# The opening of a fused attention and expert kernel: one-bank products, finer weight transfers, early first products

## Chip, cores, metric

One core of a Trainium2 chip. The metric is device time of one execution in microseconds (us). Ratios are the mean time of one kernel's fast runs over that of the kernel before in the same rounds, so they are not quite the ratios of the medians that stand beside them.

## The reference

```
q_s = softmax(q, over head dim);  k_s = softmax(k, over sequence)
x   = q_s @ (k_s^T @ v)              # batch 8, heads 8, sequence 576, head dim 64
h   = x @ w_in                       # 4608 tokens, 512 model dims, 2048 hidden columns
g   = h + sin(alpha * h)^2 / alpha
out = g @ w_out                      # (4608, 512), f32
```

Inputs are f32; the kernel multiplies in bf16.

## The kernel before

PE (TensorE) makes everything from tiles of 512 tokens: attention for a batch gives x^T; then 16 groups of 128 hidden columns ("hidden column 0 to 15" below), each four products of w_in with x^T, one per 128 model dims; then the output products from g and w_out. ACT (ScalarE) makes sines and some squares, POOL (GpSimd) and DVE (VectorE) the other squares, DVE the sums g. q, k, v of batch 0 come by SyncE's queue; the weights by POOL's queue, which casts them f32 to bf16, and behind them q, k, v of batch 1.

```python
def load_win(c0, c1):
    n = slice(c0 * 512, c1 * 512)
    for x in range(2):
        nc.gpsimd.dma_start(out=win[64 * x:64 * x + 64, :, n], in_=win_v[x][:, :, n])
...
    warm_up(14)                       # identity products, to bring the clock up
    norm_q(0, [GP, V])
    for c0, c1 in ((0, 1), (1, 2), (2, 4)):
        load_win(c0, c1)
    for c in range(3):
        load_wout(c)
    ...                               # casts of v, transposes of q
    for ii in range(2):
        kv_mm(0, ii, ps_s, split=True)
        kv_norm(0, ii, ii + 1)
    for ii in range(2):
        attn_out(0, ii, 0, ps_s, (ACT_CP, DVE_CP)[ii])
        attn_out(0, ii, 1, ps_s, (ACT_CP, DVE_CP)[ii])
        warm_up((1, 4)[ii])
...
    late = {3: ("q", q, 1, True), 6: ("k", k, 1, False), 8: ("v", v, 1, True)}
    for ni in range(nN):
        h_slot(0, ni, "PAPDPAPADPAPPDAP"[ni], lag, lent)   # A, P, D: who squares
        flush(lag, 1)                                      # DVE's sum, one behind
        if ni in late: ...            # load of batch 1, by POOL's queue
        if ni == 11:
            load_wout(3)
```

The softmax here doesn't subtract the row's maximum and nothing guards it: scores larger than these inputs give would overflow.

## Time and profile before

| | before |
|---|---|
| time, median of three runs | 293.79 us (293.63 to 294.30) |
| PE busy, share of the span | 278.9 us, 96% |
| first product of tile 0 | 17.38 us |
| last part of w_in landed | 24.20 us |
| first product of tile 1 | 49.58 us |

With a fourth run the median is 293.94, which the tables below use. PE has almost no idle time after the opening, so a change of the opening shows at the end as the shift of tile 1's first product: in all fourteen profiles of this case the span less that moment is 241.8 to 242.2 us.

### The profile page before, as it was taken

The page shows a single profiled execution, that of the slowest core. Times are in us where ns is not written, and L with a number is a line of the kernel's source. Part 1 is how long each engine was busy: PE and PEld are TensorE (multiplying, and loading weights), DVE is VectorE, ACT ScalarE, POOL GpSimd, SP SyncE. Part 2 cuts the span into 40 slices and gives each one's busy share as a digit, 9 for nine tenths or more (in the row PEclk, how much of TensorE's full clock was granted, in tenths as well). Part 3 has the DMA queues.
Part 4 walks back from the last instruction along what each step waited for, and adds up shares of the span by engine and source line. Part 5 has one row for each costly group of instructions (what it writes and reads, how often), then busy time and mean ns, then how long its engine had stood idle before and what let it go on. Part 6 is the DMA issues. An engine that isn't in the chain of part 4 may idle for free.

```text
span 291.4 us, 4261 instructions
## 1 busy us (share of the span) xinstructions
PE 278.9 (96%) x1576; PEld 132.4 (45%) x1576; DVE 188.0 (65%) x275; ACT 226.7 (78%) x320; POOL 84.9 (29%) x78
## 2 busy tenths in 40 slices
PE   2999999999999999999999999999999999999994
PEld 1444445444454445444444444445444444444444
DVE  3748955798958667855786568756774555555412
ACT  4679956999579899789987998799977777777500
POOL 0939571576684744002600070005000000000000
PEclk9999999999999999999999999999999999999999
DMA  7999999964899975109920894113411111111143
GB/s 260 294 181 207 357 254 339 395 226 130 208 139 374 393 239 117 37 23 334 290 55 14 290 292 97 36 39 70 83 38 36 36 36 38 36 36 37 38 108 73
DMA packets 35253, 45.77 MB, mean 157 GB/s; under 512 B 15888, under 2 KB 19744, under 8 KB 35232
## 3 DMA queue, kind: packets, MB, share of 16 engines
q1 hardware_dynamic: 29632, 34.09, 41.3%
q0 software_dynamic: 5408, 11.27, 15.4%
q8 instruction: 12, 0.20, 0.3%
q10 hardware_dynamic: 192, 0.14, 0.2%
q14 instruction: 9, 0.07, 0.1%
HBM read 36.71 MB, written 9.44 MB: 158 GB/s over the span
## 4 chain that ended last, share of the span: by engine, by line
PE 80%; DVE 8%; ACT 5%; POOL 3%; issue 2%; DMA 1%; ACTq 0%
PE op L255 35%; PE hp L235 31%; PE hp L255 4%; DVE g L251 3%; PE warm L299 2%; PE kvp L154 2%; POOL s L245 2%; DVE xT L215 2%; ACT s L241 2%; PE xp L212 2%; DMA st_q<-in_q_dram 1%; PE op L498 1%; PE hh L235 1%; ACT s L243 1%; DVE o L261 1%
## 5 line engine op out<-in xcount | busy, mean ns | idle before, releaser
L251 DVE SCALAR_TENSOR_TENSOR g<-s,inva_sb,hp 128x512 bf16<-128x512 f32 x130 | 95.3, 746 | 64.6 <-ACT s L243 52.1
L235 PE MATMUL hp<-xT,win 128*128 128x512 bf16 x520 | 129.5, 379 | 0.2
L255 PE MATMUL op<-wout,g 128*128 128x512 bf16 x496 | 124.0, 379 | 0.0
L241 ACT ACTIVATE s<-hp,alpha_sb 128x512 f32<-128x512 f32 x130 | 87.8, 682 | 29.4 <-PE hp L235 25.4
L235 PEld LDWEIGHTS <-win 128*128 128x128 bf16 x576 | 56.1, 98 | 68.1 <-issue 1.9
L255 PEld LDWEIGHTS <-g 128*128 128x128 bf16 x560 | 54.1, 98 | 62.6 <-issue 1.5
L243 ACT ACTIVATE s<-s 128x512 f32<-128x512 f32 x112 | 70.5, 629 | 3.6
L143 POOL TENSOR_TENSOR qn<-qe,qs 128x1152 bf16<-128x1152 bf16 x13 | 27.4, 2127 | 83.7 <-DVE qs L137 67.6
L245 POOL TENSOR_TENSOR s<-s 128x512 f32<-128x512 f32 x27 | 28.4, 1058 | 23.6 <-ACT s L241 23.4
L261 DVE COPY o<-op 128x512 f32<-128x512 f32 (+1 forms) x33 | 21.9, 664 | 10.1 <-PE op L255 7.6
L114 ACT ACTIVATE ke<-st_k 128x1152 bf16<-128x1152 f32 x16 | 17.7, 1149 | 3.2 <-DMA st_k<-in_k_dram 3.2
L114 ACT ACTIVATE qe<-st_q 128x1152 bf16<-128x1152 f32 x16 | 17.9, 1156 | 2.9 <-DMA st_q<-in_q_dram 2.9
L136 DVE TENSOR_REDUCE qs<-qe 128x36 f32<-128x2304 bf16 x5 | 12.8, 2553 | 10.8 <-ACT qe L114 10.7
L128 POOL CAST vb<-st_v 128x1152 bf16<-128x1152 f32 x14 | 16.1, 1175 | 8.7 <-DMA st_v<-in_v_dram 8.6
L215 DVE CAST xT<-xp 128x512 bf16<-128x512 f32 (+1 forms) x22 | 16.5, 752 | 2.8 <-PE xp L212 2.7
L255 PE MATMUL hp<-wout,g 128*128 128x512 bf16 x64 | 15.1, 379 | 0.4 <-DVE g L251 0.3
L212 PE MATMUL xp<-qT,kbd 128*128 128x256 bf16 (+1 forms) x56 | 10.8, 285 | 2.1 <-DVE xT L215 1.0
L154 PE MATMUL kvp<-vb,ke 64*128 64x130 bf16 x288 | 9.8, 216 | 0.5 <-ACT qT L187 0.4
L114 ACT ACT_TABLE_LOAD x7 | 9.0, 1283 | 1.3 <-PEq L514 1.2
L154 PEld LDWEIGHTS <-ke 64*128 64x128 bf16 x288 | 8.2, 93 | 3.8 <-issue 2.1
L299 PE MATMUL warm<-qe,identb 128*128 128x512 bf16 x19 | 7.4, 554 | 2.7 <-ACT qe L114 2.7
L212 PEld LDWEIGHTS <-kbd 128*128 128x128 bf16 x56 | 5.3, 97 | 9.2 <-issue 3.8
(59 smaller groups left out, 121.3 us busy)
## 6 DMA issues: line engine op xcount, KB each, us to landing
out_dram<-o SPq DMA_DIRECT2D x70, 128.0 KB, 2.4
st_q<-in_q_dram SPq DMA_DIRECT2D x5, 1152.0 KB, 6.1
st_k<-in_k_dram SPq DMA_DIRECT2D x5, 1152.0 KB, 8.7
st_v<-in_v_dram SPq DMA_DIRECT2D x5, 1152.0 KB, 10.9
st_k<-in_k_dram POOLq DMA_DIRECT2D x2, 1152.0 KB, 11.1
wout<-in_moe_w_out_dram POOLq DMA_DIRECT2D x4, 512.0 KB, 14.6
st_q<-in_q_dram SPq DMA_DIRECT2D x2, 576.0 KB, 4.4
st_k<-in_k_dram SPq DMA_DIRECT2D x2, 576.0 KB, 7.1
```

Source lines behind the costliest of these rows:

```text
L114: nc.scalar.activation(dst[:, :, ii * 128:(ii + 1) * 128].rearrange("p j (x d) -> p x j d", x=2), src[:, ii::2], AX.Exp)
L143: engs[ii % len(engs)].tensor_tensor(qn[:, ii].rearrange("p j (x d) -> p j x d", x=2), qe[:, ii], part.unsqueeze(3).to_broadcast([128, J, ...
L154: nc.tensor.matmul(kvp[:, e, ii * 130:(ii + 1) * 130], ke[r, j, ii * 128:(ii + 1) * 128], vt[r, j, ii * 130:(ii + 1) * 130], start=(j == 0 ...
L212: nc.tensor.matmul(xp[:, e, 0:n], kt[:, e, ii], qT[:, ii, j0:j1, e * 64:(e + 1) * 64], start=True, stop=True)
L215: eng(xT[:, 2 * ii:2 * ii + 2, c0:c0 + n], xp[:, :, 0:n])
L235: nc.tensor.matmul(hp, win[:, ki, ni * 128:(ni + 1) * 128], xT[:, ki, t * MF:(t + 1) * MF], start=(ki == 0), stop=(ki == 3))
L241: nc.scalar.activation(s, hp, AX.Sin, scale=alpha_sb[:, ni:ni + 1])
L243: nc.scalar.activation(s, s, AX.Square)
L245: nc.gpsimd.tensor_tensor(s, s, s, op=ALU.mult)
L251: nc.vector.scalar_tensor_tensor(G[t][:, ni], in0=s, scalar=inva_sb[:, ni:ni + 1], in1=hp, op0=ALU.mult, op1=ALU.add)
L255: nc.tensor.matmul(acc, G[t][:, ni, j * 128:(j + 1) * 128], wout[:, ni, :], start=(ni == 0), stop=(ni == nN - 1))
L261: eng(o[:, cols], acc)
```

## The change

Intent: begin the tile-0 products sooner. Batch 0's attention is made for the first 512 tokens alone, in four one-bank products (each into a PSUM tile of 128x512 f32 instead of 128x2x512), one for each quarter of the model dims; the first two hidden columns start on the first quarters while the others are still copied; w_in comes in finer column parts so that the first columns are there (`load_win` now counts columns, not blocks of 512); the squares of tile 0 are dealt out anew; and in batch 1 the last w_out chunk goes between the halves of v, whose casts move from POOL to ACT and DVE. The diff, cut to its core:

```diff
-        warm_up(14)
+    warm_up(9)
...
-        for c0, c1 in ((0, 1), (1, 2), (2, 4)):
+    for c0, c1 in ((0, 256), (256, 512), (512, 1024), (1024, 2048)):
         load_win(c0, c1)
-        for c in range(3):
+    for c in range(2):
         load_wout(c)
...
-        for ii in range(2):
-            attn_out(0, ii, 0, ps_s, (ACT_CP, DVE_CP)[ii])
-            attn_out(0, ii, 1, ps_s, (ACT_CP, DVE_CP)[ii])
-            warm_up((1, 4)[ii])
+    for c in range(4):
+        xp = ps_h.tile([128, MF], F32, name="hp", tag="h")
+        attn_chunk(0, c, 0, 8, xp)
+        (ACT_CP, ACT_CP, DVE_CP, ACT_CP)[c](xT[:, c, 0:MF], xp)
...
-        late = {3: ("q", q, 1, True), 6: ("k", k, 1, False), 8: ("v", v, 1, True)}
+        late = {3: lambda: load("q", q, 1, halves=True, eng=GP), 5: lambda: load_wout(2),
+                7: lambda: load("k", k, 1, eng=GP), 9: lambda: load_half("v", v, 1, 0, GP),
+                11: lambda: load_wout(3), 12: lambda: load_half("v", v, 1, 1, GP)}
+        for ki in range(2):
+            for ni in range(2):
+                mm_h(0, ni, lent, ki, ki + 1)
         for ni in range(nN):
-            h_slot(0, ni, "PAPDPAPADPAPPDAP"[ni], lag, lent)
+            h_slot(0, ni, "DAPPAPPDAPPDAPAP"[ni], lag, lent)
...
+        take(os, 10)
+        for c in range(4):
+            attn_chunk(0, c, 8, 9, xp[:, c])      # the last 64 tokens of batch 0
+        ACT_CP(xT[:, :, 8 * P:9 * P], xp)
+        take(os, 36)
         exp_q(1); norm_q(1, [GP, V]); exp_k(1)
-        cast_v(1, [GP_CP, GP_CP])
+        cast_v(1, [ACT_CP, DVE_CP])
```

More of the change, by code (lines that the diff above doesn't have):

```diff
@@ L94, in load, with load_half @@
         staged[name, b] = st
+    def load_half(name, t, b, ii, eng):
+        if ii == 0:
+            staged[name, b] = stage.tile([128, 4, J, D], F32, name=f"st_{name}", tag="st")
+        eng.dma_start(out=staged[name, b].rearrange("p i j d -> p i (j d)")[:, ii::2], in_=src_view(t, b)[:, ii::2])
     def load_batch(b):
@@ L101, in load_win @@
     def load_win(c0, c1):
-        n = slice(c0 * 512, c1 * 512)
+        n = slice(c0, c1)
         for x in range(2):
@@ L168, in kv_norm @@
                                     kvr[r, :, :, x].unsqueeze(3).to_broadcast([64, 2, m, D]), op=ALU.mult)
-    TP = ((0, 6), (6, 9))
     def q_tile(b):
@@ L175, in q_tile, with q_transpose @@
         return A["qT", b]
-    def q_transpose(b, g, pool, eng):
-        qn, qT = A["qn", b], q_tile(b)
-        j0, j1 = TP[g]
-        m = (j1 - j0) // 3
-        tp = pool.tile([128, 2, 2, 4, 128], BF16, name="tp", tag="a")
-        for j in range(j0, j1):
-            h, jj = divmod(j - j0, 3)
-            for ii in range(2):
-                nc.tensor.transpose(tp[:, h, ii, jj], qn[:, ii, j], identb)
-        for ii in range(2):
-            eng(qT[:, ii, j0:j1].rearrange("p (h jj) c -> p h jj c", h=m), tp[:, 0:m, ii, 0:3])
+    def q_transpose(b, ii, pool, eng):
+        tp = pool.tile([128, 16, 128], BF16, name="tp", tag="a")
+        q_transpose_ii(b, ii, 0, J, tp)
+        eng(q_tile(b)[:, ii], tp[:, 0:J])
     def q_transpose_ii(b, ii, j0, j1, tp):
@@ L224, with mm_h @@
     G = {}
-    def mm_h(t, ni, wide=None):
-        if ni == 0:
+    HP = {}
+    def mm_h(t, ni, wide=None, k0=0, k1=4):
+        if ni == 0 and k0 == 0:
             G[t] = gpool.tile([128, nN, MF], BF16, name="g")
-        if wide and ni % 6 in ((2, 3) if t == 0 else (4, 5)):
+        if k0:
+            hp = HP[t, ni]
+        elif wide and ni % 6 in ((2, 3) if t == 0 else (4, 5)):
             hp = wide()
@@ L233, in mm_h @@
             hp = ps_h.tile([128, MF], F32, name="hp", tag="h")
-        for ki in range(4):
+        HP[t, ni] = hp
+        for ki in range(k0, k1):
             nc.tensor.matmul(hp, win[:, ki, ni * 128:(ni + 1) * 128],
@@ L284 @@
         nc.vector.memset(vb[n].rearrange("p j (i c) -> p j i c", i=4)[:, :, :, D:D + 1], 1.0)
-    with tc.tile_pool(name="ps_w", bufs=1, space=PSUM) as ps_w, tc.tile_pool(name="ps_s", bufs=3, space=PSUM) as ps_s:
-        warm = ps_w.tile([128, 4, 128], F32, name="warm")
-        tpa = warm[:, 0, 0:nN]
-        nc.tensor.transpose(tpa, alpha_rows, ident[0:nN, 0:nN])
-        DVE_CP(alpha_sb, tpa)
-        nc.vector.reciprocal(inva_sb, alpha_sb)
-        exp_q(0)
-        exp_k(0)
-        def warm_up(n):
-            for _ in range(n):
-                nc.tensor.matmul(warm, identb, A["qe", 0][:, 0:4, 0:128], start=True, stop=True)
-        def cast_v0(n, eng):
-            ii, j0, j1 = VJ[n]
-            vv = vb[0].rearrange("p j (i c) -> p i j c", i=4)
-            eng(vv[:, 2 * ii:2 * ii + 2, j0:j1, 0:D], staged["v", 0][:, ii::2, j0:j1])
-        warm_up(14)
-        norm_q(0, [GP, V])
-        for c0, c1 in ((0, 1), (1, 2), (2, 4)):
-            load_win(c0, c1)
-        for c in range(3):
-            load_wout(c)
-        cast_v0(0, ACT_CP)
-        cast_v0(1, DVE_CP)
-        q_transpose(0, 0, ps_s, ACT_CP)
-        q_transpose(0, 1, ps_s, DVE_CP)
-        cast_v0(2, DVE_CP)
-        for ii in range(2):
-            kv_mm(0, ii, ps_s, split=True)
-            kv_norm(0, ii, ii + 1)
-        for ii in range(2):
-            attn_out(0, ii, 0, ps_s, (ACT_CP, DVE_CP)[ii])
-            attn_out(0, ii, 1, ps_s, (ACT_CP, DVE_CP)[ii])
-            warm_up((1, 4)[ii])
-        nc.scalar.activation(zero, zero, AX.Sin)
@@ L326 @@
-    ps_h = ctx.enter_context(tc.tile_pool(name="ps_h", bufs=4, space=PSUM, reuse_waits="tile"))
+    ps_h = ctx.enter_context(tc.tile_pool(name="ps_h", bufs=4, space=PSUM, reuse_waits="tile"))
+    ES = ExitStack()
+    ps_e = ES.enter_context(tc.tile_pool(name="ps_e", bufs=2, space=PSUM, reuse_waits="tile"))
+    tps = [ps_h.tile([128, 8, 128], BF16, name="tp", tag="h") for _ in range(3)]
+    warm = ps_h.tile([128, 4, 128], F32, name="warm", tag="h")
+    tpa = warm[:, 0, 0:nN]
+    nc.tensor.transpose(tpa, alpha_rows, ident[0:nN, 0:nN])
@@ new lines, with warm_up, cast_v0 @@
+    DVE_CP(alpha_sb, tpa)
+    nc.vector.reciprocal(inva_sb, alpha_sb)
+    exp_q(0)
+    exp_k(0)
+    def warm_up(n):
+        for _ in range(n):
+            nc.tensor.matmul(warm, identb, A["qe", 0][:, 0:4, 0:128], start=True, stop=True)
+    def cast_v0(ii, j0, j1, eng):
+        vv = vb[0].rearrange("p j (i c) -> p i j c", i=4)
+        eng(vv[:, 2 * ii:2 * ii + 2, j0:j1, 0:D], staged["v", 0][:, ii::2, j0:j1])
+    warm_up(9)
+    norm_q(0, [GP, V])
+    q_tile(0)
+    for c0, c1 in ((0, 256), (256, 512), (512, 1024), (1024, 2048)):
+        load_win(c0, c1)
@@ new lines @@
+    for c in range(2):
+        load_wout(c)
+    q_transpose_ii(0, 0, 0, 8, tps[0])
+    DVE_CP(A["qT", 0][:, 0, 0:8], tps[0])
+    cast_v0(0, 0, 5, ACT_CP)
+    cast_v0(0, 5, 9, DVE_CP)
+    warm_up(1)
+    q_transpose_ii(0, 1, 0, 8, tps[1])
+    for ii in range(2):
+        q_transpose_ii(0, ii, 8, 9, tps[2][:, ii:ii + 1])
+    ACT_CP(A["qT", 0][:, :, 8], tps[2][:, 0:2])
+    cast_v0(1, 0, 5, DVE_CP)
+    ACT_CP(A["qT", 0][:, 1, 0:8], tps[1])
+    cast_v0(1, 5, 9, ACT_CP)
+    for ii in range(2):
+        kv_mm(0, ii, ps_e, split=True)
+        kv_norm(0, ii, ii + 1)
@@ L328, in h_slot @@
+    for c in range(4):
+        xp = ps_h.tile([128, MF], F32, name="hp", tag="h")
+        attn_chunk(0, c, 0, 8, xp)
+        (ACT_CP, ACT_CP, DVE_CP, ACT_CP)[c](xT[:, c, 0:MF], xp)
+    nc.scalar.activation(zero, zero, AX.Sin)
     def h_slot(t, ni, sq, lag, wide=None):
-        hp = mm_h(t, ni, wide)
+        hp = mm_h(t, ni, wide, 2 if t == 0 and ni < 2 else 0)
         lag.append((t, ni, hp, sine(t, ni, hp, sq)))
@@ L356 @@
     SQ = "PAPDPAPAPPDPAPAP"
-    with tc.tile_pool(name="ps_e", bufs=2, space=PSUM, reuse_waits="tile") as ps_e:
+    with ES:
         def lent():
             return ps_e.tile([128, 2, MF], F32, name="hh", tag="a")[:, 0]
-        late = {3: ("q", q, 1, True), 6: ("k", k, 1, False), 8: ("v", v, 1, True)}
+        late = {3: lambda: load("q", q, 1, halves=True, eng=GP), 5: lambda: load_wout(2),
[4 more added lines that the diff above has]
+                mm_h(0, ni, lent, ki, ki + 1)
         for ni in range(nN):
-            h_slot(0, ni, "PAPDPAPADPAPPDAP"[ni], lag, lent)
+            h_slot(0, ni, "DAPPAPPDAPPDAPAP"[ni], lag, lent)
             flush(lag, 1)
             if ni in late:
-                name, x, b, hv = late[ni]
-                load(name, x, b, halves=hv, eng=GP)
-            if ni == 11:
-                load_wout(3)
+                late[ni]()
         flush(lag, 0)
+        accs = [ps_h.tile([128, dm], F32, name="hp", tag="h") for _ in range(4)]
+        os = o_quad(0, accs, [DVE_CP, ACT_CP, DVE_CP, ACT_CP])
+        take(os, 10)
+        xp = ps_e.tile([128, 4, P], F32, name="xp", tag="a")
+        for c in range(4):
+            attn_chunk(0, c, 8, 9, xp[:, c])
+        ACT_CP(xT[:, :, 8 * P:9 * P], xp)
+        take(os, 36)
         exp_q(1)
@@ L374 @@
         exp_k(1)
-        cast_v(1, [GP_CP, GP_CP])
+        cast_v(1, [ACT_CP, DVE_CP])
         for name, x in (("q", q), ("k", k), ("v", v)):
             load(name, x, 2, eng=GP)
-        accs = [ps_h.tile([128, dm], F32, name="hp", tag="h") for _ in range(4)]
-        os = o_quad(0, accs, [DVE_CP, ACT_CP, DVE_CP, ACT_CP])
-        take(os, 44)
         q_transpose(1, 0, ps_e, ACT_CP)
         nc.scalar.activation(zero, zero, AX.Sin)
-        take(os, 2)
         q_transpose(1, 1, ps_e, DVE_CP)
```

## The prediction

> **What bounds the kernel now.** I read the page first: TensorE (PE) is busy in 96% of the span, in every slice of forty but the first and the last, and the chain that ended last lies 80% on PE. So a gain in the opening is kept to the end only if PE's stream from there on starts earlier. Tile 1 and everything after it has the same instructions in both kernels; the quantity to predict is therefore the moment at which the first product of tile 1 starts, 49.58 us in the profile. Next I read PE's timeline of the opening (start, length, engine, line, what, count, idle before it):
>
> ```profile
> 5.89 5.97 PE L299 MATMUL warm<-qe,identb 128*128 128x512 bf16 x14 [2.66 <-ACT qe L114]
> 11.70 1.17 PE L185 MATMUL tp<-identb,qn 128*128 128x128 bf16 x18
> 12.80 1.54 PE L154 MATMUL kvp<-vb,ke 64*128 64x130 bf16 x36
> ...
> 17.38 1.89 PE L235 MATMUL hp<-xT,win 128*128 128x512 bf16 x8
> 19.10 1.89 PE L235 MATMUL hh<-xT,win 128*128 128x512 bf16 x8
> 20.83 3.62 PE L235 MATMUL hp<-xT,win 128*128 128x512 bf16 x16
> 24.34 1.89 PE L235 MATMUL hh<-xT,win 128*128 128x512 bf16 x8
> ...
> 33.90 7.71 PE L255 MATMUL hp<-wout,g 128*128 128x512 bf16 x35 [0.28 <-DVE g L251]
> ```
>
> The tile-0 products run from 17.38 to 31.24 with no gap of note (64 matmuls at 0.216 us are 13.8 us). It looks as if an earlier start at 17.38 would pay. But the weight loads of the same line, asked for around 24 us, and the view of the w_in tile tell another story:
>
> ```profile
> 23.85 0.10 PEld L235 LDWEIGHTS <-win 128*128 128x128 bf16 x1
> 24.31 0.34 PEld L235 LDWEIGHTS <-win 128*128 128x128 bf16 x3 [0.36 <-issue]
> ```
>
> ```profile
> L104 POOL DMA_DIRECT2D win<-in_moe_w_in_dram x6: 640/661/787, 9.8 to 13.0; - x6
> ...
> DMA to landing us min/median/max: 4.5/7.2/11.2
> ```
>
> The last of six w_in transfers is issued at 13.0 and takes 11.2 us: it lands at 24.2. Hidden column 8 x 128 is the first that needs it, and its weights load at 24.31, 0.1 us after the landing, where the load had the weight path idle for 0.36 us. PE lost only about 0.06 us there, so products and w_in arrive together: PE has no slack against the transfer. The slices of 2 us (length, busy time and count of PE, PEld, DVE, ACT, POOL, then clock, DMA share, GB/s) say why w_in comes so late:
>
> ```profile
> 8.00:10.00 2.00, 2.00 (x6) 0.72 (x5) 1.93 (x3) 1.26 (x2) 2.00 (x2) 1.00 1.05 388
> ...
> 14.00:16.00 2.00, 1.50 (x18) 0.92 (x16) 1.34 (x5) 0.99 (x3) 1.87 (x3) 1.00 1.16 141
> 16.00:18.00 2.00, 1.85 (x10) 0.74 (x9) 1.42 (x2) 1.74 (x3) 0.00 (x0) 1.00 1.09 168
> 18.00:20.00 2.00, 2.00 (x11) 0.91 (x10) 0.00 (x0) 1.37 (x2) 0.79 (x1) 1.00 1.17 215
> ```
>
> The DMA share is about 1 or over in all of them. The weights are counted as bf16 written; their f32 source is twice that, so 205 GB/s written is some 410 read, the same rate as q, k and v before them. By the landings in the trace the queue stays full from w_in through two w_out chunks, the third, batch 1's q, k, v (41.3) and the last w_out chunk (43.67). Batch 1's kv products start at 43.88 and end at 45.07; attn_out follows at 46.31, tile 1 at 49.58. The opening is as much a DMA queue of 41 us as a PE stream.
>
> **What the Trainium skill says.** "DMA: Bandwidth & Descriptors", section "Issuing engines are not separate DMA queues": all transfers share 16 engines whoever issues them. The trace agrees: no rate over about 410 GB/s read, from either queue. Same page, "Why small descriptors are slow (HBM only)": a fixed cost per packet. The packet records agree: 2048 B written took 173 ns, 1024 B took 98, so the fixed part is about 23 ns. "TensorE: Matmul & The Clock Gate", Part 1: half clock until a window of about 3.4 us was busy. In the trace the warm-up products are 426 ns apart until the clock goes to full at 11.57, 5.7 us after the first. "ScalarE: Activation LUTs", "What ACT_TABLE_LOAD costs": 1283 ns; the trace has 1283 too, before the first sine.
>
> **The change part by part.**
>
> *Start of the products.* Five fewer warm-ups take 5 x 0.426 = 2.1 us from PE's queue (9.73 instead of 11.86), so transposes start when qn's halves are there (9.82 and 11.03). v's first half lands at 11.40, its second at 12.27 and 13.01. With casts of 0.44 to 0.7 us split over ACT and DVE, and the long qT copy on ACT ahead of its last cast (13.4 to 13.9), kv of the second half ends near 14.3, kv_norm 0.75 later at 15.05. Four one-bank attention products and four copies of 0.6 to 0.7 us give x^T's quarters at 15.2, 15.8, 16.2 and 16.4. Products of the first model dims start near 15.5, and by 17.1 the first two hidden columns are done, which is 2.0 us ahead of before (17.38 + 1.73 = 19.11). ACT gains only 0.5: its copy still ends at 16.4, the table load takes 1.28, so the first sine comes at 17.9 rather than 18.44.
>
> *w_in parts.* The bytes are the same and the first issue is where it was, behind POOL's normalisation (9.76). The first quarter of the columns now goes in packets of 512 B, about 60 ns each by the two measured sizes: with the overlap seen at 1024 B that is 168 instead of 205 GB/s, so 0.5 MB takes 3.1 us instead of 2.6. The first two hidden columns can be had near 14.3 (w_in's first pair was 15.79), which suits the early start. But columns 1024 to 2048 remain the last pair: 24.2 plus up to 0.5. PE, 2 us early, waits for the second group about 0.9 us near 19 and for the third to 24.3-24.8. The last eight hidden columns are 8 x 0.863 = 6.9 us, so tile 0 ends at 31.2 to 31.8 instead of 31.24. The 2 us do not survive.
>
> *Tile 0's tail.* ACT and DVE catch up during those waits, and the last squares are no longer DVE's (one took 1.48 us beside POOL): the 0.28 us wait at 33.9 goes. Four 64-column products for the last 64 tokens cost 0.2. Before, 44 output products were done at 41.6; now 46 at 41.4 to 42.0: +0.1 to -0.5 in all.
>
> *Batch 1.* The third w_out chunk moves behind q, so q lands 2.5 us earlier, but its exp waits for the extra copy and table load, about 35.5, later than the 33.84 of before; qn is still there (near 41.8) when its transposes come. v's second half is now last in the queue, behind the last w_out chunk. The queue's end was 43.67; call the new landing L. Its cast moves from POOL (1.2 us) to DVE (0.75 by 0.44 for 512 and 0.50 for 640 columns), then in DVE's order the 1152-column qT copy (0.9) and kv_norm (1.1): attention products can start at L + 2.85 and tile 1 3.27 after that (46.31 to 49.58 before), so at L + 6.1. That equals 49.58 at L = 43.5. With L = 43.67 plus 0 to 0.5 the change loses 0.2 to 0.7; PE's own stream, if L were not the limit, would gain about 0.5 at most at the same w_in landing.
>
> Sum: +0.2 to +0.7 us, of 293.8. Against it I set one thing the trace does not explain: from 14.5 to 16.7 the same 1024 B packets took up to 172 ns, while POOL issued the w_out chunks. One chunk fewer is issued there now. If that stretch of low rate shrinks, the whole queue comes up to 1.2 us earlier, and everything with it. I take half a microsecond for it, and a little more for the reordering having been tuned: -0.2 in all, 293.6.
>
> **The rivals.**
> *The opening gain goes through.* If the tile-0 products' 2 us were kept, 291.8. For it: PE's gapless stream and the chain, which names the warm-ups. Against: the landing at 24.2 beside the load at 24.31.
> *The finer parts cost more.* Packets of 512 B at 98 ns would halve the rate of the first quarter: +2.6 us on the queue, so 296. Against it: the source f32 rows are 1 KB, and packets of q and v of that size on the other queue took 50 ns.
> *The clock stays at half.* With nine warm-ups the window to 11.57 holds short gaps (before qn's first half, before its second). If the rise comes 3.4 us later, transposes, kv and attention take about 1.5 us more. But that eats into the 2 us that w_in hides anyway: 293.6 to 294.
> *v's second half delays kv.* That is the L of above; a tail of 1 us on it gives 294.8.
>
> **Range and chances.** The best case (queue 1.2 us earlier and no tail) is about 292.2, the worst that I believe (finer packets at half rate, less something) about 295.4. I give 292.0 to 295.4. Two per cent is 5.9 us, more than a third of the 17.4 us before the first product: hardly in reach either way. Faster 0.03, same 0.95, slower 0.02.
>
> **What would show it.** Right: products start near 15.5; PE idles before hidden columns 4 to 8; the last w_in part lands at 24 or later; tile 0 ends between 31 and 32; kv of batch 1 waits on the DVE cast of v's second half; tile 1 starts within 1 us of 49.6. Wrong: the last w_in landing well before 24, tile 0 over by 30, or no wait at batch 1's kv.

## The result, and the profile after

295.32 us median (295.16 to 295.75, four runs) against 293.94 for the kernel before: ratio 1.0049, 95% interval 1.0031 to 1.0066. Within 2%, inside the stated range, but slower by 1.4 us where the prediction had a gain of 0.2. The two profiled executions differ by 2.6 us of span (294.0 and 291.4), 1.2 us more than the medians: the one of after was the slowest of its four, the one of before faster than all its timed runs. Sizes below that come from single profiles carry a doubt of that order.

PE's timeline after (start, length, engine, line, what, count, idle before it and who ended it); compare with the first fence of the prediction (hp and hh are PSUM tiles from two pools, L236 here is L235 before; a row is eight products for two hidden columns, or sixteen for four, with a record missing here and there):

```profile
5.93 3.82 PE L304 MATMUL warm<-qe,identb 128*128 128x512 bf16 x9 [2.66 <-ACT qe L119]
...
15.51 1.89 PE L236 MATMUL hp<-xT,win 128*128 128x512 bf16 x7
17.23 1.89 PE L236 MATMUL hh<-xT,win 128*128 128x512 bf16 x8
21.46 3.61 PE L236 MATMUL hp<-xT,win 128*128 128x512 bf16 x16 [2.34 <-DMA win<-in_moe_w_in_dram]
26.46 1.89 PE L236 MATMUL hh<-xT,win 128*128 128x512 bf16 x8 [1.39 <-DVE g L252]
...
34.27 2.10 PE L256 MATMUL hp<-wout,g 128*128 128x512 bf16 x9 [0.28 <-DVE g L252]
...
46.08 1.20 PE L159 MATMUL kvp<-vb,ke 64*128 64x130 bf16 x36 [0.23 <-ACT qT L183]
...
51.79 3.62 PE L236 MATMUL hp<-xT,win 128*128 128x512 bf16 x16
```

The products do start at 15.51. Then PE stands still twice, 2.34 us before hidden column 4 and 1.39 before column 8, and tile 1 starts 2.21 us later than before. The second wait is put down to DVE, but the sum of hidden column 2, whose buffer column 8 takes over, had ended at 22.10; the one that ended just before the wait's end (26.35) is of column 5. The weight loads (same columns) and the view of the w_in tile point to the true releaser:

```profile
26.43 0.56 PEld L236 LDWEIGHTS <-win 128*128 128x128 bf16 x4 [1.85 <-issue]
```

```profile
L109 POOL DMA_DIRECT2D win<-in_moe_w_in_dram x8: 630/648/842, 9.8 to 14.4; - x8
DMA to landing us min/median/max: 3.4/5.7/11.9
```

The last of eight transfers is issued at 14.4 and takes 11.9 us: it lands at 26.33 by the trace, 0.1 us before the load. Before, the landing was at 24.20. That is 2.13 us, and tile 1 is 2.21 us late: nearly all of the opening's loss has the size of this one landing. The slices of 2 us (columns as in the prediction; the last number is GB/s written) show where the queue lost it:

```profile
12.00:14.00 2.00, 1.24 (x36) 0.92 (x30) 1.24 (x5) 1.70 (x3) 2.00 (x4) 1.00 1.28 159
14.00:16.00 2.00, 1.63 (x12) 0.58 (x8) 1.27 (x4) 1.37 (x3) 2.00 (x4) 1.00 0.98 103
16.00:18.00 2.00, 1.95 (x10) 0.92 (x10) 0.18 (x1) 1.97 (x4) 0.58 (x1) 1.00 0.86 106
18.00:20.00 2.00, 1.12 (x6) 0.29 (x3) 1.55 (x3) 1.97 (x4) 0.00 (x0) 1.00 1.17 198
```

From 14 to 18 us, 103 and 106 GB/s against 141 and 168 before. There is a second sign in the semaphore records. Each transfer raises its semaphore 16 times in these traces, once for each DMA engine, and is taken as landed at the last. For the last w_in part the first and last reports are at 23.22 and 24.20 before, at 24.04 and 26.33 after: there twelve reports had come by 24.76, and the last four came at 25.49 to 26.33.

### The profile page after: what moved, and what is told of

It reads as the page before. It is cut to its first block, busy times and chain, and to the rows that moved or that the text cites. A ratio compares the mean times of both kernels' runs of the same rounds, so it can differ in the third digit from the quotient of the medians.

```text
span 294.0 us, 4215 instructions
## 1 busy us (share of the span) xinstructions
PE 274.8 (93%) x1539; PEld 130.9 (45%) x1567; DVE 189.4 (64%) x273; ACT 227.7 (77%) x323; POOL 84.4 (29%) x78
## 4 chain that ended last, share of the span: by engine, by line
PE 73%; DVE 9%; DMA 5%; POOL 4%; ACT 4%; issue 4%; POOLq 0%; ACTq 0%
PE op L256 31%; PE hp L236 30%; PE hp L256 5%; DMA win<-in_moe_w_in_dram 3%; DVE g L252 3%; ACT s L242 2%; POOL s L246 2%; DVE xT L211 2%; PE kvp L159 2%; PE xp L208 2%; DVE o L262 1%; DMA qT<-qn 1%; DMA st_q<-in_q_dram 1%; DVE qs L146 1%; PE op L515 1%
## 5 line engine op out<-in xcount | busy, mean ns | idle before, releaser
L236 PE MATMUL hp<-xT,win 128*128 128x512 bf16 x510 | 128.7, 379 | 3.0 <-DMA win<-in_moe_w_in_dram 2.3
L256 PE MATMUL op<-wout,g 128*128 128x512 bf16 x480 | 121.5, 379 | 1.1 <-issue 0.5
L236 PEld LDWEIGHTS <-win 128*128 128x128 bf16 x576 | 56.0, 98 | 71.8 <-issue 5.6
L211 DVE CAST xT<-xp 128x512 bf16<-128x512 f32 (+1 forms) x20 | 15.1, 753 | 2.1 <-PE xp L208 2.0
L133 POOL CAST vb<-st_v 128x1152 bf16<-128x1152 f32 x12 | 13.6, 1163 | 7.6 <-DMA st_v<-in_v_dram 4.0
L208 PE MATMUL xp<-qT,kbd 128*128 128x256 bf16 (+1 forms) x48 | 9.5, 285 | 1.6 <-DVE xT L211 1.0
L236 PE MATMUL hh<-xT,win 128*128 128x512 bf16 x40 | 9.4, 379 | 1.4 <-DVE g L252 1.4
L146 DVE TENSOR_REDUCE qs<-qe 128x18 f32<-128x1152 bf16 x6 | 7.9, 1322 | 4.2 <-ACT qe L119 4.2
L119 ACT ACT_TABLE_LOAD x7 | 9.0, 1283 | 1.3 <-PEq L531 1.2
```

What stands on the lines that cost most here:

```text
L119: nc.scalar.activation(dst[:, :, ii * 128:(ii + 1) * 128].rearrange("p j (x d) -> p x j d", x=2), src[:, ii::2], AX.Exp)
L208: nc.tensor.matmul(xp[:, e, 0:n], kt[:, e, ii], qT[:, ii, j0:j1, e * 64:(e + 1) * 64], start=True, stop=True)
L211: eng(xT[:, 2 * ii:2 * ii + 2, c0:c0 + n], xp[:, :, 0:n])
L236: nc.tensor.matmul(hp, win[:, ki, ni * 128:(ni + 1) * 128], xT[:, ki, t * MF:(t + 1) * MF], start=(ki == 0), stop=(ki == 3))
L256: nc.tensor.matmul(acc, G[t][:, ni, j * 128:(j + 1) * 128], wout[:, ni, :], start=(ni == 0), stop=(ni == nN - 1))
```

## The experiments

Names beginning with "a" are edits of the changed kernel, with "b" of the kernel before. All gave correct results. Landing and start are of the profiled execution.

| run | median us | ratio to before (95%) | last w_in landed | tile 1 starts |
|---|---|---|---|---|
| before | 293.94 | 1 | 24.20 | 49.58 |
| the change | 295.32 | 1.0049 (1.0031 to 1.0066) | 26.33 | 51.79 |
| a_coarse_win | 293.93 | 1.0005 (0.998 to 1.003) | 24.27 | 50.33 |
| a_hold_products | 296.04 | 1.0077 (1.0055 to 1.0098) | 25.92 | 52.14 |
| a_wout_later | 296.06 | 1.0082 (1.0058 to 1.0105) | 26.28 | 53.10 |
| a_batch1_as_before | 294.91 | 1.0044 (1.0019 to 1.007) | 26.56 | 51.82 |
| b_fine_win | 295.56 | 1.0071 (1.0048 to 1.0093) | 26.67 | 52.05 |
| a_even_win | 293.85 | 1.0007 (0.999 to 1.0024) | 24.79 | 50.13 |
| a_csplit_win | 294.96 | 1.0054 (1.0029 to 1.008) | 25.90 | 51.37 |
| a_even_batch1 | 293.31 | 0.9989 (0.9974 to 1.0004) | 24.26 | 49.70 |
| a_even_tuned | 293.72 | 0.9998 (0.9983 to 1.0012) | 24.50 | 49.95 |
| a_even_oldsq | 293.17 | 0.9979 (0.9962 to 0.9996) | 24.63 | 49.31 |
| b_swap_win | 295.71 (one run) | none | 24.46 | 51.79 |
| a_oldsq_hold | 294.91 | 1.0028 (1.0012 to 1.0044) | 24.90 | 51.94 |

**Where is the loss?** Theory 1: the finer parts. Theory 2: the w_out transfers issued right behind. Theory 3: batch 1's order. And whether the early start is worth anything.

*a_coarse_win.*

```diff
-    for c0, c1 in ((0, 256), (256, 512), (512, 1024), (1024, 2048)):
+    for c0, c1 in ((0, 512), (512, 1024), (1024, 2048)):
```

> The changed kernel with w_in in the three parts of before (512, 512, 1024 columns); all else as changed. Theory 1, the finer parts are what makes the last w_in part land late (26.33 us against 24.20): the last part lands near 24.2 again, tile 0 ends near 31.3, and the time falls by about 2 us below the changed kernel, to 293.3 or so, 0.5 below before. Theory 2, the late landing comes of where the w_out transfers are issued or of chance on the DMA engines and not of the part size: the last part lands at 25.5 or later and the time stays within 0.5 us of the changed kernel's 295.3. Theory 3, the cost is in batch 1's order: the landing may move, the time stays at 295.

The view of the w_in tile, and PE at hidden column 8:

```profile
DMA to landing us min/median/max: 4.4/7.3/11.3
```

```profile
24.41 1.89 PE L236 MATMUL hh<-xT,win 128*128 128x512 bf16 x8 [1.32 <-DMA win<-in_moe_w_in_dram]
```

Issued at 12.95, landed at 24.27: theory 1's landing to the tenth. The time fell by 1.4 us to that of before, not to 0.5 below it: the ratio is 1.0005. So the finer parts are the loss, and something else eats the gain; in this profile PE waits 0.41 and 0.28 us for DVE at 32.2 and 32.8, the latter also in the kernel before, and tile 1 still starts 0.75 us later than there.

*a_hold_products.*

```diff
+    warm_up(9)
     for c in range(4):
         xp = ps_h.tile([128, MF], F32, name="hp", tag="h")
         attn_chunk(0, c, 0, 8, xp)
```

> The changed kernel with nine more warm-up products (1.9 us) ahead of the four attention products of tile 0, which puts the early start of the tile-0 products back by about 1.9 us. Theory (w_in is the limit, the early start is hidden): PE's wait before hidden column 4 shrinks from 2.3 us to about 0.4 and the time stays within 0.3 us of the changed kernel's 295.3. Rival (the early start is worth something): the time rises by 1 to 1.9 us to over 296.3.

Products at 17.36 instead of 15.51; PE no longer waits before column 4, still to 26.06 before column 8. By the ratios the time rose by 0.3% (0.8 us), between the two expectations; the intervals of 1.0077 and 1.0049 overlap, and by their widths the rise may be anything from nothing to about 1.6 us (an estimate). In the two profiles the last eight products of tile 0 start at 31.66 and 31.64, and tile 1 at 52.14 and 51.79. (The profile here is of the fastest of its four runs, that of the change of the slowest, so their equal ends say nothing.) With the finer parts the early start of 1.85 us is mostly hidden: 0.35 us of it shows in the profiles.

*a_wout_later.*

```diff
-    for c in range(2):
-        load_wout(c)
...
-        late = {3: lambda: load("q", q, 1, halves=True, eng=GP), 5: ...
+        late = {2: lambda: load_wout(0), 3: lambda: load_wout(1),
+                4: lambda: load("q", q, 1, halves=True, eng=GP), 5: ...
```

> The changed kernel with the two front w_out transfers issued after hidden columns 2 and 3 and batch 1's q after column 4, so that POOL issues nothing between 15 and 20 us. Theory 2 (the slow stretch of the queue from 15 to 17.5 us comes of POOL's issuing of w_out): packets of 1024 B take about 98 ns there, the last w_in part lands at 24.5 or before, tile 0 ends near 31.5 and the time is 293.3 to 293.9. Rival (part size or chance): the stretch stays slow, the landing stays at 26 and the time at 295.3 or above.

The slices show the slow stretch as it was, with POOL (the fifth pair of numbers) issuing nothing after 14.85 us and idle from 16 us on:

```profile
14.00:16.00 2.00, 1.13 (x11) 0.45 (x11) 0.81 (x4) 1.19 (x3) 0.85 (x2) 1.00 1.08 122
16.00:18.00 2.00, 2.00 (x11) 0.90 (x10) 0.69 (x1) 1.87 (x3) 0.00 (x0) 1.00 1.11 145
```

The landing is 26.28. Theory 2 is out. The ratio rose to 1.0082, though the intervals overlap. In the profile the queue ran low from 23 to 26 us (138, 141 and 179 GB/s in the three, against 205, 198 and 208 in the changed kernel): w_out landed later, v's second half at 47.06, and the second half of batch 1's kv waited 0.47 us for its cast. It is the only one of these runs in which that wait of the prediction showed.

*a_batch1_as_before.*

```diff
-    for c in range(2):
+    for c in range(3):
         load_wout(c)
...
+        late = {3: lambda: load("q", q, 1, halves=True, eng=GP), 6: lambda: load("k", k, 1, eng=GP),
+                8: lambda: load("v", v, 1, halves=True, eng=GP), 11: lambda: load_wout(3)}
...
-        cast_v(1, [ACT_CP, DVE_CP])
+        cast_v(1, [GP_CP, GP_CP])
```

> The changed kernel with the order of transfers of before (three w_out chunks up front, q, k, v whole, then the last w_out chunk) and v of batch 1 cast on POOL. Theory 1 and 2 (the loss sits in w_in's landing, before any of this): the time stays within 0.4 us of the changed kernel's 295.3. Theory 3 (v's second half at the queue's end costs): it falls by 1 us or more, to 294.3 or below.

1.0044 against 1.0049: no difference within the noise, and w_in again lands late, at 26.56. Theory 3 is out.

**The harm by itself, and what kind of part does it.**

*b_fine_win* puts the four finer parts alone into the kernel before.

```diff
-        for c0, c1 in ((0, 1), (1, 2), (2, 4)):
+        for c0, c1 in ((0, 256), (256, 512), (512, 1024), (1024, 2048)):   # in columns
```

> The kernel before with one thing of the change alone: w_in in the four finer parts. Theory 1 (packets of 512 B leave some DMA engines behind, whatever the opening does): the last w_in part lands at 25.9 to 26.6 us, PE waits near 2 us before hidden column 8, and the time rises by 1.5 to 2.3 us, to about 295.5. Rival (the late landing needs the new opening beside it): the part lands before 24.8 and the time rises by less than 0.6.

```profile
26.81 1.89 PE L235 MATMUL hh<-xT,win 128*128 128x512 bf16 x8 [1.67 <-DMA win<-in_moe_w_in_dram]
```

Landed at 26.67, ratio 1.0071, 2.0 us by the medians. One line of the change, alone, gives all of its loss, with the old opening and the old start of the products.

*a_even_win.*

```diff
-    for c0, c1 in ((0, 256), (256, 512), (512, 1024), (1024, 2048)):
+    for c0, c1 in ((0, 512), (512, 1024), (1024, 1536), (1536, 2048)):
```

> The changed kernel with w_in in four parts of 512 columns. If packets of 1024 B keep the DMA engines together, columns 1024 to 1535 land near 22 us and the rest near 24.3; PE's wait of 1.3 us before hidden column 8 (seen with three parts) falls under 0.4, and the time comes to 292.8 to 293.3, below before. Rival 1 (the small packets are again the harm): the last part lands at 25 or later, time 294 or more. Rival 2 (ACT, DVE and POOL bound tile 0's tail anyway): the landing is good and PE's wait goes, but the time stays at 293.7 to 294.1.

```profile
23.25 1.89 PE L236 MATMUL hh<-xT,win 128*128 128x512 bf16 x8
24.98 1.89 PE L236 MATMUL hp<-xT,win 128*128 128x512 bf16 x8
27.93 1.89 PE L236 MATMUL hp<-xT,win 128*128 128x512 bf16 x7 [1.06 <-DVE g L252]
```

Rival 2 came true. Again eight transfers, but each of 256 KB in bf16: landing at 24.79, no wait before column 8 (23.25), and then PE waits 1.06 us at column 12 for a buffer that DVE's sum holds. The time is that of a_coarse_win. Once w_in is on time, what PE waits for in tile 0 is DVE's sums, which follow the sines and squares.

*a_csplit_win.*

```diff
-    for c0, c1 in ((0, 256), (256, 512), (512, 1024), (1024, 2048)):
-        load_win(c0, c1)
+    for d in (slice(0, 2), slice(2, 4)):       # model dims, two quarters at a time
+        load_win(0, 512, d)
+    for c0, c1 in ((512, 1024), (1024, 2048)):
+        load_win(c0, c1)
```

> The changed kernel with its eight w_in transfers, but columns 0 to 511 cut by model dims (two of four at a time) instead of by columns, so the same number and size of transfers in packets of 1024 B. Theory 1a (packet size is the harm): last landing 24.2 to 24.6, time 293.7 to 294.2 as with three parts. Theory 1b (the number of transfers is the harm): last landing 25.9 or later, time 295 or more.

By its landing theory 1b: 25.90, ratio 1.0054, though no data packet of w_in had under 1024 B. So it is not the packet size. Nor is it the bare number of transfers, for a_even_win has eight as well. What the late kernels share is four transfers of 128 KB at the head of the queue, and the table of all runs bears it out: in the six profiles that have them the last part landed at 25.90 to 26.67 and the queue wrote 103 to 145 GB/s from 16 to 18 us; in the eight without, 24.20 to 24.90 and 166 to 188.

*a_even_batch1* adds to a_even_win the batch-1 edit shown above.

> Four parts of 512 columns and the order of transfers and POOL casts of before, in the changed kernel: the new opening without the rest. If POOL's transfer issues between its squares hold up tile 0's tail, this is 0.3 to 0.7 us faster than the run with four even parts alone; if they do not, the two agree within 0.3 us.

0.9989 against 1.0007, about 0.5 us, as expected if POOL's issues hold up the tail. But the intervals overlap, and the edit moves transfers and casts as well, so this is not shown; the next run speaks against it.

**Tile 0's tail, and the slow stretch.**

*a_even_tuned.*

```diff
-            h_slot(0, ni, "DAPPAPPDAPPDAPAP"[ni], lag, lent)
+            h_slot(0, ni, "DAPPAPPDADPPAPAD"[ni], lag, lent)
...             and load_wout(3) after column 13 instead of 11
```

> The run a_even_batch1 with tile 0's squares dealt out anew (the square of hidden column 9 from POOL to DVE, 11 from DVE to POOL, 15 from POOL to DVE) and the last w_out chunk issued after column 13 instead of 11, so that no square waits behind POOL's issue of v. If POOL's issues hold up DVE's sums and so PE's buffers in tile 0 (waits of 0.23, 0.41, 0.40 and 0.28 us in a_even_batch1), two or three of these waits go and the time falls by 0.5 to 1.0 us, to 0.994 to 0.997 of before. Rival (ACT's sines and squares are the bound there): within 0.2 us of a_even_batch1, 0.998 to 1.000 of before.

A miss: 0.9998, not faster. The four waits (1.32 us) did not go, they gathered in two: 0.41 us before column 12 and 0.92 us at 34.2 (1.33 us). So POOL's issues were not what set the sum of them.

*a_even_oldsq.*

```diff
-            h_slot(0, ni, "DAPPAPPDAPPDAPAP"[ni], lag, lent)
+            h_slot(0, ni, "PAPDPAPADPAPPDAP"[ni], lag, lent)
```

> The run a_even_batch1 with the squares of tile 0 dealt out as before the change. If the new deal of squares is what gives the waits of PE on DVE in tile 0's tail, the time falls by 0.3 us or more below a_even_batch1 (under 0.998 of before); if the deal is indifferent or better, the time is the same or up to 0.5 us more, 0.999 to 1.001.

0.9979 (0.9962 to 0.9996): the best of all runs and the only one whose interval lies under 1, by little, and one of twelve intervals, so a real gain over the kernel before is likely rather than certain. PE's timeline in tile 0's end:

```profile
30.00 1.93 PE L256 MATMUL hp<-wout,g 128*128 128x512 bf16 x8
32.26 0.38 PE L256 MATMUL hp<-wout,g 128*128 128x512 bf16 x1 [0.33 <-DVE g L252]
32.92 0.38 PE L256 MATMUL hp<-wout,g 128*128 128x512 bf16 x1 [0.28 <-DVE g L252]
33.58 0.28 PE L216 MATMUL xp<-qT,kbd 128*128 128x64 bf16 x4 [0.28 <-DVE g L252]
...
49.31 2.97 PE L236 MATMUL hp<-xT,win 128*128 128x512 bf16 x13
```

Tile 0's products are done at 30.00 where the kernel before had 31.24, and 0.9 us of the 1.2 are then spent waiting for DVE's sums (0.28 in the kernel before); tile 1 starts 0.27 us earlier. Its lead over a_even_batch1 is inside the intervals.

*b_swap_win* is slower on purpose.

```diff
-        for c0, c1 in ((0, 1), (1, 2), (2, 4)):
+        for c0, c1 in ((1, 2), (0, 1), (2, 4)):
```

> The kernel before with the first two w_in parts in the other order (columns 512 to 1023 first). It is slower on purpose (the first products wait for the second part). Looked at: the packets of 1024 B between 14.5 and 16.7 us. If the slow stretch belongs to the addresses of columns 512 to 1023, it comes at 11 to 13.5 us and packets from 14.5 on take 98 ns; if it belongs to the time or to the place in the queue, it stays at 14.5 to 16.7 with 50 to 60 packets in half a microsecond.

The packets stay slow from 15.0 to 16.5 us: 67, 54 and 58 in half a microsecond, against 96 to 103 at full rate; at 13.5 to 14.5 they are fast. So, by this one profile, the stretch does not belong to those addresses.

*a_oldsq_hold* is a_even_oldsq with the nine warm-up products of a_hold_products.

> The best run so far (a_even_oldsq, 0.998 of before) with nine more warm-up products ahead of tile 0's attention products, so that the products start 1.9 us later, near where they started before the change. There w_in is not what PE waits for. If the early start is worth its length once w_in comes in even parts, the time rises by 1.3 to 1.9 us, to 1.003 of before or more; if DVE's tail of tile 0 takes most of it (waits of 0.33, 0.28 and 0.28 us that would shrink), it rises by 0.3 to 0.9 us, to 0.999 to 1.001 of before; if it is worth nothing, it stays at 0.998.

1.0028 against 0.9979, with intervals apart (the two are compared through the kernel before): 0.49% of 294 is 1.4 us. With w_in in even parts the early start is worth about 1.4 of its 1.9 us. (In this profile, the slowest of the six runs, the products came at 18.09, 2.1 us later than in a_even_oldsq.) With the start put back the rebuilt opening is 0.8 us slower than the kernel before. How much of that the rest of the rebuilding costs is not shown, for in the profile the start came 0.7 us later than the 17.38 of before.

## Why the prediction was right or wrong

The outcome lay in the range because the main reason held: w_in's landing, not the start of the products, sets tile 0's end. It is shown by PE's waits, by a_coarse_win and b_fine_win, by a_hold_products in part and, turned round, by a_oldsq_hold, where the same hold costs 1.4 us once w_in comes evenly. But the centre had the wrong sign, and the outcome lay in the range by only 0.08 us, under an upper end taken from a rival (512 B packets at half rate) that did not happen: that much is luck. Of the prediction's own signs, the early products, PE's waits before columns 4 and 8 and a landing after 24 came true; tile 0's products ended after 33 instead of between 31 and 32, kv did not wait on DVE's cast, and tile 1 was 2.2 us off instead of within 1. The working shows which terms did it.

- *Start of the products*: right. 15.51 against "near 15.5", the first sine at 17.71 against 17.9. The clock went up at 9.45 us (8.65 to 11.77 over the fourteen profiles), so that rival fell.
- *w_in parts*: **the step that failed.** "But columns 1024 to 2048 remain the last pair: 24.2 plus up to 0.5." It was 26.33. The term itself was worked out from packet sizes, and packets of 512 B did take 60 ns as estimated; the 512 columns that they carried landed at 15.69, where the kernel before had them at 15.79. The loss came in the transfers behind them: the slow stretch became deeper (103 and 106 GB/s instead of 141 and 168) and left some engines behind. Small transfers at the head of the queue do this by themselves (b_fine_win, a_csplit_win); small packets are not needed. The rival "the finer parts cost more" came near the size (2.6 us on the queue; the landing moved by 2.1), by the wrong mechanism.
- *The allowance for the slow stretch*: wrong. I took half a microsecond off because one w_out chunk fewer is issued there. a_wout_later has none issued there, and the stretch is there all the same. The reading behind it was loose as well: 172 ns is the mean of half a microsecond. By the packet records the median packet of 1024 B took 98 ns in that stretch as elsewhere, and single ones took up to 989 ns; in the changed kernel up to 1318. The stretch is some packets that stall, not all packets slowed. (Nor was about 410 GB/s the top rate: the prediction's own 215 GB/s written is 430 read.) This allowance, and the trust that the order had been tuned, turned a sum of +0.2 to +0.7 into -0.2.
- *Tile 0's tail*: wrong in kind. "The 0.28 us wait at 33.9 goes": it is still there, at 34.27, and with w_in on time more such waits appear. ACT and DVE do not catch up; DVE's squares still took 1.63 and 1.68 us when a POOL square ran beside them, against 0.69 alone. The Trainium skill has this in "GPSIMD Engine Reference", Specifications: the SBUF interfaces are shared with VectorE, and instructions with two SBUF inputs contend. I had moved the squares in my head without looking up that cost.
- *Batch 1*: right in that the order changes little (a_batch1_as_before), wrong in the wait. v's second half landed at 45.10, 1.4 us after the 43.67 of before instead of 0 to 0.5 (43.57 in a_coarse_win, with w_in on time). Its cast took 0.76 us as worked out and ended at 45.88, but kv had to wait until 46.08 for ACT's copy of qT anyway, so L was close to the limit and not it. And the exp of batch 1's q, put at "about 35.5", began at 38.32 (36.86 in a_coarse_win).

What stays open: why the DMA queue slows between 14.5 and 17.5 us in every one of these kernels, and why four transfers of 128 KB make it slow down more. Shown are four things that it is not: the issue of w_out, the addresses of columns 512 to 1023, the size of the packets, and the rebuilt opening beside it (b_fine_win). How the 16 engines share such transfers was not measured. One rival was not tested: in the changed kernel POOL took 0.63 to 0.84 us to issue a w_in transfer, small or large, so the four small ones were handed over at about 200 GB/s (an estimate: 128 KB in 0.65 us), no faster than the queue's 198 to 215 after the stretch, and no stock could build up behind them. Against it, the last of w_in had been issued by 15.08 and the queue was still slow after 16.

## What to carry to other kernels

Before bringing products forward, look for what lands just in time behind them: here a weight load 0.1 us after a landing said that an earlier start could not reach the end. Cutting a transfer to get its first piece sooner can delay the pieces behind it; cut the late part, which PE waits for as a whole, and leave the head of the queue in large transfers (here 256 KB against 128). After removing the wait on a transfer, expect the next bound (here DVE's sums, which hold the PSUM buffers) at nearly the same place: only 0.2% was left of a gain of 1.9 us at the start.

## What the Trainium skill lacked or had wrong

- "DMA: Bandwidth & Descriptors" tells of small transfers that they carry more fixed cost. It lacks that four transfers of 128 KB (bf16) at the head of a busy POOL queue delay the ones behind: the last w_in part landed 1.7 to 2.5 us later (25.90 to 26.67 against 24.20), and the 16 engines' reports for one transfer spread over 2.0 to 3.2 us in the kernels with them, 0.9 to 1.6 in those without.
- The same page has no packet times for POOL's casting transfers: 512 B written took 60 ns, 1024 B 98, 2048 B 173.
- "TensorE: Matmul & The Clock Gate" says that the clock falls after an idle window of about 3.4 us, and to avoid gaps of over some 3 us. In a_batch1_as_before a gap of 2.3 us (19.4 to 21.7) was enough: the clock was at half from 21.97 for 3.4 us. In the changed kernel a gap of the same length had no such effect in the profile. A reading of these two cases, not a rule: the clock changes of a_batch1_as_before (11.73, 21.97, 25.38) lie 10.24 and 3.41 us apart, as on a fixed grid of 3.41 us. On it PE worked 1.1 us in the stretch that ended at 21.97. In the changed kernel the grid from its rise at 9.45 would cut the gap in two and leave 1.6 us of work in the emptier stretch.

The slices of a_batch1_as_before that show the fall (the number after POOL's count is the granted clock):

```profile
19.40:21.70 2.30, 0.00 (x1) 0.03 (x1) 1.48 (x3) 1.65 (x3) 1.15 (x2) 1.00 1.15 209
21.97:25.38 3.41, 3.41 (x10) 1.22 (x9) 1.77 (x3) 1.62 (x3) 2.06 (x3) 0.50 1.15 208
```

- "ScalarE: Activation LUTs" adds a drain of about 1380 ns to each table load of 1283. In these traces the load (1283 ns) starts 0.02 us after the copy before it and the next activation follows it directly (16.31 plus 1.28, then 17.60): no drain is seen.
